# Retention and two wide feed-forward layers on one core: moving the first layer's float64 loads to GpSimd's queue, and three smaller moves of loads and operand making

## The chip, the cores and the metric

The kernel runs on one core of a Trainium2 chip. The metric is device time in microseconds, start to end of one execution on that core. Engine names are those of the profile: PE is TensorE (matmul) and PEld its weight loads, DVE is VectorE, ACT is ScalarE, POOL is GpSimd, and SP is SyncE, which here only issues DMAs. A DMA that SP or ACT issues goes out on queue q1 or q10 of the profile, a DMA that POOL issues on q0.

## The reference

```python
# q, k, v: 4 x 8 x 768 x 64 float32; x: 3072 tokens x 512; w_in 512 x 2048, w_out 2048 x 512 in float64
gamma = 1.0 - 2.0 ** (-5.0 - np.arange(H))
for t in range(S):                                   # retention, per batch and head
    state = gamma * state + k[t] (outer) v[t]
    y[t] = q[t] @ state / sqrt(64)
x = y.transpose(0, 2, 1, 3).reshape(3072, 512)
h = x @ moe_w_in;  x = (h * sigmoid(1.702 * h)) @ moe_w_out
h = x @ moe2_w_in; x = square(max(h, 0)) @ moe2_w_out
```

## The kernel before

**Retention.** The 3072 tokens are 24 units of 128 tokens. `load_unit` brings one unit as two transfers of 512 KB from SP's queue into one of four buffers (`UNITS = 4`). In iteration u the loop runs `scores(u)` on PE (16 matmuls), `outputs(u - 1)` (yp, dp and the matmuls with the state), then `cv_step`, and last issues the load of unit u + 3, whose buffer is free once `outputs(u - 1)` has read unit u - 1. `masked` (pt) and `scaled` (x) are the two DVE operations that each unit needs. Of the six blocks of 512 tokens, block 0 is split into hi and lo parts at once, blocks 1 to 3 stay in SBUF (`XHELD = 4`), and blocks 4 and 5 go to a DRAM tensor `xkept`, one store of 256 KB per unit from POOL's queue.

**The first layer's weights.** They come as float64 words: 32 slices (`order`) of 512 KB. A slice is a load into one of three `raw` buffers (`cv_load`, line 114, SP's queue), a scaling on ACT (`cv_a`, tile `hm`), and a chain of five or six DVE operations with one ACT copy (`cv_step`, lines 152 to 176) that leaves the tile `w` with a hi and a lo part. The load of slice n + 3 needs the buffer of slice n and so waits for that slice's last DVE operation, line 176. Some slices are made in the retention, the others beside block 0 of the first layer.

**The first layer, blocks 0 to 3** (`NSTD = 4`). For each of 16 column groups f, `up` runs 12 matmuls into `h`, ACT makes `gs` and `gh`, DVE makes `gl` (line 590), and `down` of the group two earlier (`LOOK = 2`) runs 12 matmuls into `y`. Beside blocks 1 to 3, `background(BG)` gives a generator (`maker`) a credit per group, in estimated us of DVE: it makes the operands of the second half of the program, 16 sets of sums from the first layer's weights (`make_first`, tiles `wh`) and 32 jobs on the second layer's float64 weights (`make_second`, tiles `w`, `hm`, `wq`, stored to `kw` by POOL). In block 3 the generator `x_operands` also runs, one step per group from f = 5 on: it makes the operands `xh`, `xl` of the first seven-product block.

**Seven-product blocks.** The last third of the first layer and all of the second run as four blocks of 1024 tokens with seven products in place of eight (`up2`, `down2`; L748 is their matmul). Their weight tiles `r` come by SP's queue in 256 KB loads from `kw`, each used by six matmuls, up to eight ahead (`SLOTS = 8`, of which two are free before block 3 ends). At the start of each block `x_loads` loads the next block's x (four transfers of 512 KB on POOL's queue, line 623); `up2` calls `background(BGUP)` 14 times.

All orders of work are written out by hand: an engine runs its instructions in the order in which the program issues them, and so does each queue.

Of the kernel before, what the change touches and what calls it, by code (L numbers as in the profile page):

```python
# [18 lines left out]
P = 128  # L19
# [21 lines left out]
SLOTS = 8  # L41
EARLY = 2
BG = 4.3
BGUP = 2.0

# [7 lines left out]
def tile_retention_then_two_ffns(  # L55
# [22 lines left out]
        ctx.enter_context(tc.tile_pool(name=f"wr{i}", bufs=1, side="right", reuse_waits="tile"))  # L78
        for i in range(EARLY)
    ]  # L80
    cv_ctx = ctx.enter_context(ExitStack())
    cv_p = cv_ctx.enter_context(tc.tile_pool(name="cv", bufs=2, side="right"))
    maker_ctx = ctx.enter_context(ExitStack())
# [20 lines left out]
    def cv_load():  # L104
        n = cv["load"]
        if n == len(order):
            return
        if n >= cv["b"] + 3:
            return
        cv["load"] += 1  # L110
        f, s = order[n]
        raw = cv_p.tile([P, 512, 2], U32, tag="raw", name=f"raw{n}", bufs=3)
        src = w1[f, :, s * 512:(s + 1) * 512].bitcast(U32)
        nc.sync.dma_start(out=raw, in_=src.rearrange("p (c t) -> p c t", t=2))
        cvt[n] = [raw]

    def cv_a():
# [230 lines left out]
            yield from low(*last)  # L348

    def make():  # L350
        cv_ctx.close()
        raw_p.append(maker_ctx.enter_context(
            tc.tile_pool(name="k0", bufs=2, side="right", reuse_waits="tile")
        ))
        yield from make_first()
        yield from make_second()
# [36 lines left out]
    with tc.manual_schedule():  # L393

        with (
# [13 lines left out]
            table_sb = att.tile([P, 1], F32, tag="table", name="table_sb", bufs=1)  # L409
            nc.scalar.activation(out=table_sb, in_=warm_sb[:, 0:1], func=ACTF.Gelu_apprx_sigmoid)  # L410


            x0_sb = [att.tile([P, NP, P], F32, tag="x0", name="x0_0")]
            st_sb = [att.tile([P, NP, P], F32, tag=f"st{i}", name=f"st{i}", bufs=1) for i in range(2)]
            for t in st_sb:
                nc.gpsimd.memset(t, 0.0)
# [67 lines left out]
            def outputs(u):  # L484
                t = units.pop(u)
                pt, vs = pend.pop(u)
                b, c = divmod(u, CPB)
                qk = t[:, 0:1024].rearrange("p (b n a i) -> p b n a i", b=2, n=2, a=2)
                kn = t[:, 1024:1536].rearrange("p (h e) -> p h e", h=H)
                yp = aps.tile([P, NP, P], F32, tag="yp", name=f"yp{u}")  # L490
                for p in range(NP):
                    for r in range(2):
                        nc.tensor.matmul(  # L493
                            yp[64 * r:64 * r + 64, p, :], vs[:, 2 * p + r, :], pt[:, r, p, :],
                            start=(p == 0), stop=(c == 0), skip_group_check=True,
                        )
                dp, st = state.pop(b, (None, None))
                if c == 0:
                    dp = aps.tile([P, 2, NP, D], F32, tag="dp", name=f"dp{b}")
                if c < CPB - 1:  # L500
                    for p in range(NP):
                        for r in range(2):
                            nc.tensor.matmul(
                                dp[64 * r:64 * r + 64, 0, p, :], kn[:, 2 * p + r, :], vs[:, 2 * p + r, :],
                                start=(c == 0 and p == 0), stop=(c == CPB - 2), skip_group_check=True,
                            )
                    ns = st_sb[u % 2]
                    for r in range(2):
                        h = slice(64 * r, 64 * r + 64)
                        nc.scalar.copy(out=ns[h, :, h], in_=dp[h, 0])  # L510
                    state[b] = (dp, ns)
                if c > 0:
                    for p in range(NP):
                        nc.tensor.matmul(
                            yp[:, p, :], st[:, p, :], qk[:, p // 2, 0, p % 2, :],
                            start=False, stop=True, skip_group_check=True,
                        )
                j, o = divmod(u, UPB)
                cols = slice(o * P, (o + 1) * P)
                if 0 < j < XHELD and o == 0:  # L520
                    xs[j] = block_tiles(f"x{j}")

                def scaled():
                    if 0 < j < XHELD:
                        for i in range(2):
                            pair = slice(2 * i, 2 * i + 2)
                            v.tensor_tensor(
                                out=xs[j][i][:, :, cols], in0=yp[:, pair], in1=ytab_sb[c][:, pair], op=ALU.mult
                            )
                        return  # L530
                    xt = x0_sb.pop() if x0_sb else att.tile([P, NP, P], F32, tag="x0", name=f"x0_{u}")
                    v.tensor_tensor(out=xt, in0=yp, in1=ytab_sb[c], op=ALU.mult)
                    if j == 0:
                        pend["x"] = (xt, cols)
                    else:
                        nc.gpsimd.dma_start(out=xkept[j][:, :, cols], in_=xt)

                return scaled

# [9 lines left out]
            for u in range(NU + 1):  # L549
                masked = scores(u) if u < NU else None  # L550
                split_0()
                scaled = outputs(u - 1) if u > 0 else None
                if 0 < u < CPB:
                    for p in range(NP):
                        nc.scalar.mul(ytab_sb[u][:, p, :], ytab_sb[0][:, p, :], ystep_sb[:, u, p:p + 1])
                cv_step(2 * WA if u >= 3 and u % 2 != 1 or u == 3 else 0, masked, scaled, u >= 2)
                if u > 0:
                    load_unit(u + UNITS - 1)

# [13 lines left out]
        def up(n, f):  # L573
            hi, lo = weights(f, 0)
            hp = hp_p.tile([P, TB], F32, tag="h", name=f"h{n}_{f}")
            for k in range(KD):
                xh, xl = hl[n][k]
                nc.tensor.matmul(hp, lo[:, k], xh, start=(k == 0), stop=False)  # L578
                nc.tensor.matmul(hp, hi[:, k], xh, start=False, stop=False)  # L579
                nc.tensor.matmul(hp, hi[:, k], xl, start=False, stop=(k == KD - 1))  # L580
            g = g_p.tile([P, TB], F32, tag="gs", name=f"gs{n}_{f}", bufs=1)
            gh = g_p.tile([P, TB], F32R, tag="gh", name=f"gh{n}_{f}")
            gl = g_p.tile([P, TB], F32R, tag="gl", name=f"gl{n}_{f}")

            nc.scalar.activation(out=g, in_=hp, func=ACTF.Gelu_apprx_sigmoid)  # L585
            nc.scalar.copy(out=gh, in_=g)  # L586
            gs[n, f] = (gh, gl)

            def low():
                v.tensor_tensor(out=gl, in0=g, in1=gh, op=ALU.subtract)  # L590

            if n == 0:
                cv_step(len(order), None, low)
                if f % 3 == 2:
                    cv_step()
            else:
                low()
                if f < NF - 1:
                    background(BG)

        def down(n, f):
            hi, lo = weights(f, 1)
# [99 lines left out]
        for n in range(NSTD):  # L702
            for f in range(NF):
                up(n, f)
                if f >= LOOK:
                    down(n, f - LOOK)
                elif n > 0 and f == 0:
                    down(n - 1, NF - 1)
                    finish(n - 1)
                if f == 2 and XHELD - 2 <= n < NSTD - 2:  # L710
                    xs[n + 2] = load_block(f"x{n + 2}", xkept[n + 2])
                if n == NSTD - 1:
                    if f == 3:
                        gen = x_operands(*x_loads(*blocks[0]))
                    if f >= 5:
                        next(gen, None)
                    if f == NF - 3:
                        fetch()
            down(n, NF - 2)
            if n + 1 < NSTD:  # L720
                split_x(n + 1, xs.pop(n + 1))
# [25 lines left out]
        def matmul(a, w, b, start, stop):  # L747
            nc.tensor.matmul(a, w, b, start=start, stop=stop, skip_group_check=True)  # L748

        def up2(l, n, first):  # L750

            xb, yb, zb = {}, {}, {}
            late = deque()
# [24 lines left out]
                    v.scalar_tensor_tensor(out=t, in0=t, scalar=0.0, in1=t, op0=ALU.max, op1=ALU.mult)  # L778

            for p in range(NQ + 1):  # L780
                if p < NQ:
                    xb[p] = bank(f"X{l}_{n}_{p}")
                    product(1, p, xb[p][0], True)
                    copy(gt(11, p), xb[p][0])
                else:
                    next(first)
# [156 lines left out]

        for k, (l, n) in enumerate(blocks):
            todo.extend((i, m) for i in ORDER for m in range(NQ // 2))
            gen = iter(())
            if k + 1 < len(blocks):
                gen = x_operands(*x_loads(*blocks[k + 1]))
            rest = down2(l, n, lambda: next(gen, None))
            up2(l, n, rest)  # L950
            for _ in rest:
                pass
            for _ in gen:
                pass
            if (l, n) == (1, 0):
                assert next(maker, 0) == 0 and not acts
# [82 lines left out]
```

## Time and profile before

| | us |
|---|---|
| runs shown (3): lowest, median, highest | 1087.12, 1088.05, 1088.72 |
| the profiled execution: its own time | 1089.05 |
| its span, first to last instruction | 1087.3 |
| PE busy | 1057.3 |
| DVE busy | 795.3 |
| ACT busy | 512.2 |
| POOL busy | 83.7 |

The profiled execution took 1.0 us more than the median of the runs, and its span is 1.75 us shorter than its own time. PE busy is time in which at least one matmul is under way; at a lower clock the same matmul is busy for longer.

### The profile page before, as it was taken

Reading aid. Unit: us, or ns where it says so; the run is one execution under the profiler, and the core shown is the slowest. Engines: PE = TensorE matmul, PEld = TensorE weight load, DVE = VectorE, ACT = ScalarE, POOL = GpSimd, SP = SyncE. Lnnn points to the kernel's source line nnn. Section 1 sums busy time; section 2 is a strip of 40 time slices with the busy share of each in tenths; the row PEclk is TensorE's granted clock in tenths of the full one; section 3 lists DMA queues with packets and bytes.
Section 4 is the critical chain, followed back from the end, with each engine's and each line's share of the span. In section 5 each row is a group of like instructions: output and inputs, shape, how many; then the busy total and the mean of one; then the engine's idle time right before and its main releaser. Section 6 shows DMA issues by size and latency. Waiting matters only on the chain.

```text
span 1087.3 us, 15308 instructions
## 1 busy us (share of the span) xinstructions
PE 1057.3 (97%) x5482; PEld 875.9 (81%) x5482; DVE 795.3 (73%) x1197; ACT 512.2 (47%) x862; POOL 83.7 (8%) x117
## 2 busy tenths in 40 slices
PE   7888999999999999899999999999999999999998
PEld 6877887888888888778888878888888888888886
DVE  3877998869798789945788667698444888355953
ACT  4877554434444445444546433446323455224443
POOL 2001000011111121110000110000100000000000
PEclk8999999999999999989999999999999999999999
DMA  8898445986466596599966798766876667767664
GB/s 310 300 328 297 156 136 169 385 336 228 180 215 221 165 337 211 195 344 327 308 208 206 236 334 273 210 214 205 260 244 195 194 210 232 215 193 194 195 211 165
DMA packets 107004, 259.34 MB, mean 239 GB/s; under 512 B 11312, under 2 KB 11440, under 8 KB 106928
## 3 DMA queue, kind: packets, MB, share of 16 engines
q1 hardware_dynamic: 83696, 173.42, 49.9%
q0 software_dynamic: 18048, 67.12, 17.0%
q10 hardware_dynamic: 5184, 17.83, 5.0%
q8 instruction: 44, 0.72, 0.3%
q14 instruction: 32, 0.26, 0.1%
HBM read 184.91 MB, written 73.40 MB: 238 GB/s over the span
## 4 chain that ended last, share of the span: by engine, by line
PE 82%; DMA 9%; DVE 6%; ACT 1%; issue 1%; SPq 0%; POOL 0%; DVEq 0%; ACTq 0%; POOLq 0%
PE D L748 28%; PE X L748 15%; PE Z L748 7%; PE h L578 4%; PE y L610 4%; PE h L580 4%; PE h L579 4%; PE y L609 4%; PE y L608 4%; DMA unit<-qkv 4%; PE Y L748 4%; DMA r<-kw 3%; PE yp L493 1%; PE sc L444 1%; DMA raw<-win 1%
## 5 line engine op out<-in xcount | busy, mean ns | idle before, releaser
L748 PE MATMUL D<-gx,r 128*128 128x512 f32 x1344 | 306.4, 389 | 0.0
L748 PEld LDWEIGHTS D<-gx,r 128*128 128x128 f32 x1344 | 252.0, 188 | 53.0 <-DVE gx L849 0.8
L849 DVE TENSOR_TENSOR gx<-g,gx 128x1024 fp32r<-128x1024 f32 x112 | 136.5, 1221 | 36.9 <-ACT gx L848 36.7
L748 PE MATMUL X<-xh,r 128*128 128x512 f32 x512 | 159.0, 392 | 3.2 <-DMA r<-kw 3.2
L848 ACT CAST gx<-g 128x1024 fp32r<-128x1024 f32 x112 | 116.7, 1053 | 92.9 <-PE D L748 83.3
L769 ACT COPY g<-X 128x512 f32<-128x512 f32 x96 | 56.5, 588 | 186.7 <-PE X L748 186.7
L774 DVE TENSOR_TENSOR g<-Z,g 128x512 f32<-128x512 f32 x64 | 44.2, 691 | 126.8 <-ACT g L769 92.3
L748 PEld LDWEIGHTS X<-xh,r 128*128 128x128 f32 x512 | 96.0, 189 | 26.1 <-issue 2.5
L610 PE MATMUL y<-gl,w 128*128 128x512 f32 x256 | 100.7, 393 | 3.2 <-DVE gl L590 3.2
L578 PE MATMUL h<-hl,w 128*128 128x512 f32 x256 | 99.8, 390 | 1.9 <-DVE w L176 1.9
L608 PE MATMUL y<-gh,w 128*128 128x512 f32 x256 | 100.3, 392 | 0.0
L609 PE MATMUL y<-gh,w 128*128 128x512 f32 x256 | 100.3, 392 | 0.0
L748 PE MATMUL X<-xl,r 128*128 128x512 f32 x256 | 99.9, 390 | 0.0
L579 PE MATMUL h<-hl,w 128*128 128x512 f32 x256 | 99.6, 389 | 0.0
L580 PE MATMUL h<-hl,w 128*128 128x512 f32 x256 | 99.6, 389 | 0.0
L748 PE MATMUL Z<-xh,r 128*128 128x512 f32 x256 | 79.0, 390 | 0.3 <-DMA r<-kw 0.3
L586 ACT CAST gh<-gs 128x512 fp32r<-128x512 f32 x64 | 40.0, 624 | 62.1 <-PE y L609 61.3
L585 ACT ACTIVATE gs<-h 128x512 f32<-128x512 f32 x64 | 38.2, 597 | 56.5 <-PE h L580 37.3
L590 DVE TENSOR_TENSOR gl<-gs,gh 128x512 fp32r<-128x512 f32 x64 | 44.0, 688 | 27.8 <-ACT gh L586 27.5
L610 PEld LDWEIGHTS y<-gl,w 128*128 128x128 f32 x256 | 48.5, 190 | 13.6 <-DVE gl L590 3.6
L578 PEld LDWEIGHTS h<-hl,w 128*128 128x128 f32 x256 | 48.1, 188 | 12.2 <-DVE w L176 2.3
L609 PEld LDWEIGHTS y<-gh,w 128*128 128x128 f32 x256 | 48.5, 189 | 10.2
(103 smaller groups left out, 1586.5 us busy)
## 6 DMA issues: line engine op xcount, KB each, us to landing
r<-kw SPq DMA_DIRECT2D x448, 256.0 KB, 3.0
kw<-wq POOLq DMA_DIRECT2D x32, 896.0 KB, 6.2
unit<-qkv SPq DMA_DIRECT2D x47, 512.0 KB, 7.3
raw<-w SPq DMA_DIRECT2D x32, 512.0 KB, 3.7
kw<-wh POOLq DMA_DIRECT2D x16, 1024.0 KB, 5.1
kw<-w SPq DMA_DIRECT2D x16, 512.0 KB, 6.5
raw<-win ACTq DMA_DIRECT2D x16, 512.0 KB, 5.1
raw<-wout ACTq DMA_DIRECT2D x16, 512.0 KB, 5.4
```

What stands on the lines that cost most here:

```text
L578: nc.tensor.matmul(hp, lo[:, k], xh, start=(k == 0), stop=False)
L579: nc.tensor.matmul(hp, hi[:, k], xh, start=False, stop=False)
L580: nc.tensor.matmul(hp, hi[:, k], xl, start=False, stop=(k == KD - 1))
L590: v.tensor_tensor(out=gl, in0=g, in1=gh, op=ALU.subtract)
L608: nc.tensor.matmul(a, lo[:, e], gh, start=s0, stop=False)
L609: nc.tensor.matmul(a, hi[:, e], gh, start=False, stop=False)
L610: nc.tensor.matmul(a, hi[:, e], gl, start=False, stop=s1)
L748: nc.tensor.matmul(a, w, b, start=start, stop=stop, skip_group_check=True)
L769: nc.scalar.copy(out=t, in_=a)
L774: v.tensor_tensor(out=t, in0=a, in1=t, op=ALU.add)
L848: nc.scalar.copy(out=hi, in_=src)
L849: v.tensor_tensor(out=lo, in0=src, in1=hi, op=ALU.subtract)
```

## The change

- The loads of the first layer's float64 slices are issued by POOL instead of SP.
- Units 5 and 9 of the retention get a slice to make as well; beside block 0 the extra slices come after groups 3, 6 and 9 in place of 2, 5, 8, 11 and 14.
- Blocks 4 and 5 of x are kept in SBUF (`xout`) in the retention; two stores of 1 MB each, at groups 2 and 3 of block 0, take the place of eight of 256 KB.
- The next block's x is loaded in the middle of the up projection of a seven-product block (p = 4 of 8), not at the block's start.
- In block 3 of the first layer, groups 5 to 14 give `maker` a credit of 2.9 in place of 4.3; `BGUP` is 2.3 in place of 2.0.

```diff
-BGUP = 2.0
+BGUP = 2.3
...
+    keep_ctx = ctx.enter_context(ExitStack())
+    keep_p = keep_ctx.enter_context(tc.tile_pool(name="keep", bufs=1, side="right"))
+    xout = {j: keep_p.tile([P, KD, TB], F32, tag=f"xo{j}", name=f"xout{j}") for j in range(XHELD, NT // TB)}
...
-        nc.sync.dma_start(out=raw, in_=src.rearrange("p (c t) -> p c t", t=2))
+        nc.gpsimd.dma_start(out=raw, in_=src.rearrange("p (c t) -> p c t", t=2))
...
     def make():
+        while cv["b"] < len(order):
+            cv_step()
         cv_ctx.close()
+        keep_ctx.close()
...
-                        return
-                    xt = x0_sb.pop() if x0_sb else att.tile([P, NP, P], F32, tag="x0", name=f"x0_{u}")
-                    v.tensor_tensor(out=xt, in0=yp, in1=ytab_sb[c], op=ALU.mult)
-                    if j == 0:
+                    elif j > 0:
+                        v.tensor_tensor(out=xout[j][:, :, cols], in0=yp, in1=ytab_sb[c], op=ALU.mult)
+                    else:
+                        xt = att.tile([P, NP, P], F32, tag="x0", name=f"x0_{u}")
+                        v.tensor_tensor(out=xt, in0=yp, in1=ytab_sb[c], op=ALU.mult)
                         pend["x"] = (xt, cols)
-                    else:
-                        nc.gpsimd.dma_start(out=xkept[j][:, :, cols], in_=xt)
...
-                cv_step(2 * WA if u >= 3 and u % 2 != 1 or u == 3 else 0, masked, scaled, u >= 2)
+                cv_step(2 * WA if u >= 3 and (u % 2 != 1 or u in (3, 5, 9)) else 0, masked, scaled, u >= 2)
...
                 cv_step(len(order), None, low)
-                if f % 3 == 2:
+                if f in (3, 6, 9):
                     cv_step()
...
-                    background(BG)
+                    background(BG if n < NSTD - 1 or f < 5 else BG - 1.4)
...
+                if n == 0 and f in (2, 3):
+                    j = XHELD + f - 2
+                    nc.gpsimd.dma_start(out=xkept[j], in_=xout[j])
...
-        def up2(l, n, first):
+        def up2(l, n, first, loads):
...
             for p in range(NQ + 1):
+                if p == NQ // 2:
+                    loads()
...
-            gen = iter(())
-            if k + 1 < len(blocks):
-                gen = x_operands(*x_loads(*blocks[k + 1]))
-            rest = down2(l, n, lambda: next(gen, None))
-            up2(l, n, rest)
+            gen = [iter(())]
+
+            def loads():
+
+                if k + 1 < len(blocks):
+                    gen[0] = x_operands(*x_loads(*blocks[k + 1]))
+
+            rest = down2(l, n, lambda: next(gen[0], None))
+            up2(l, n, rest, loads)
```

PE's order is the same instruction for instruction. On SP, early in the retention, the queue before has the slice loads (`raw`, L114) among the units' (L435):

```order
L435 DMA unit_225<-qkv 128x1024 x2
L114 DMA raw_278<-w 128x1024
L114 DMA raw_280<-w 128x1024
L435 DMA unit_282<-qkv 128x1024 x2
L114 DMA raw_337<-w 128x1024
L435 DMA unit_339<-qkv 128x1024 x2
L114 DMA raw_403<-w 128x1024
```

In the change SP's queue holds units alone there (L440 is the same line), and POOL's queue has the slice loads among the multiplications of V (`vs`, units 2 to 5), which POOL does for the first six units:

```order
L468 TENSOR_TENSOR vs_243<-unit_172,tab_sb 128x512
L118 DMA raw_283<-w 128x1024
L118 DMA raw_285<-w 128x1024
L468 TENSOR_TENSOR vs_300<-unit_175,tab_sb 128x512
L118 DMA raw_342<-w 128x1024
L468 TENSOR_TENSOR vs_357<-unit_230,tab_sb 128x512
L118 DMA raw_408<-w 128x1024
L468 TENSOR_TENSOR vs_423<-unit_287,tab_sb 128x512
L118 DMA raw_476<-w 128x1024
```

So nothing but units waits on SP now, and the slice loads wait behind one another on POOL. On DVE, at the end of block 3, before the change one job of `maker` (`w`, `hm`, `wq`) stands between the `gl` of two groups; these rows are from group 13's `gl` to group 14's (`xl` is the step of `x_operands`):

```order
L590 TENSOR_TENSOR gl_13_4315<-gs_13_4313,gh_13_4314 128x512
L342 TENSOR_TENSOR w_21_4238<-w_21_4238 128x128
L343 TENSOR_TENSOR w_21_4238<-w_21_4238 128x128
L318 TENSOR_SCALAR w_22_4325<-hm_22_4237 128x512
L323 SCALAR_TENSOR_TENSOR w_22_4325<-hm_22_4237,w_22_4325 128x512
L327 TENSOR_SCALAR hm_22_4237<-w_22_4325 128x512
L329 SCALAR_TENSOR_TENSOR hm_22_4237<-raw_22_4272,hm_22_4237 128x512
L637 TENSOR_TENSOR xl_4105<-xb_2_1_0_3858,xh_4104 128x1024
L590 TENSOR_TENSOR gl_14_4365<-gs_14_4363,gh_14_4364 128x512
```

and with the change, from group 14's `gl` to group 15's, the last that PE waits for before the seven-product blocks:

```order
L594 TENSOR_TENSOR gl_14_4322<-gs_14_4320,gh_14_4321 128x512
L333 SCALAR_TENSOR_TENSOR hm_20_4197<-raw_20_4189,hm_20_4197 128x512
L301 TENSOR_TENSOR wq_4281<-w_19_4198,wq_4281 128x7x128
L340 TENSOR_TENSOR w_20_4283<-w_20_4283,hm_20_4197 128x512
L343 TENSOR_TENSOR w_20_4283<-w_20_4283 128x128
L344 TENSOR_TENSOR w_20_4283<-w_20_4283 128x128
L642 TENSOR_TENSOR xl_4253<-xb_2_0_0_3848,xh_4252 128x1024
L594 TENSOR_TENSOR gl_15_4362<-gs_15_4360,gh_15_4361 128x512
```

By the end of block 3 `maker` has come to job 20 in place of job 23; the jobs left over are made in the seven-product blocks.

## Rows read from the trace of the kernel before

**Rows 1.** Busy us (instructions) by stretch of PE, PEld, DVE, ACT, POOL; clock; DMA share; GB/s.
```profile
0.00:50.00 50.00, 40.72 (x518) 34.86 (x520) 30.55 (x61) 29.81 (x96) 7.80 (x13) 0.90 0.86 306
50.00:100.00 50.00, 41.89 (x600) 38.11 (x596) 37.86 (x65) 36.86 (x124) 2.99 (x4) 0.93 0.93 323
...
300.00:400.00 100.00, 100.00 (x443) 82.81 (x442) 84.80 (x173) 46.42 (x72) 17.32 (x20) 1.00 0.67 221
```

**Rows 2.** PE's waits over the span: for what, us in total, times, longest.
```profile
PE sc L444 <- DMA unit<-qkv: 14.0, 7, 3.9
PE y L610 <- DVE gl L590: 3.2, 1, 3.2
PE X L748 <- DMA r<-kw: 3.2, 8, 1.0
PE h L578 <- DVE w L176: 1.9, 1, 1.9
```

**Rows 3.** Waits of SP's queue from 0 to 115 us: the largest.
```profile
SPq L114 <- DVE w L176: 47.2, 10, 8.2
```

**Rows 4.** SP's issues in order of time: start us, us, queue and line.
```profile
30.96 0.33 SPq L114 DMA_DIRECT2D raw<-w  x1
31.38 2.05 SPq L435 DMA_DIRECT2D unit<-qkv  x4
```

**Rows 5.** Busy time by stretch, as Rows 1, 10 us each in the retention.
```profile
20.00:30.00 10.00, 9.43 (x150) 8.65 (x152) 7.91 (x18) 8.28 (x27) 2.44 (x3) 1.00 0.96 366
30.00:40.00 10.00, 7.63 (x96) 6.72 (x93) 9.36 (x19) 7.23 (x26) 0.00 (x0) 0.90 0.80 273
```

**Rows 6.** DMA from 0 to 110 us: totals; POOL's stores with time to landing.
```profile
DMA packets 9664, 34.03 MB, mean 309 GB/s; under 512 B 1097, under 2 KB 1225, under 8 KB 9650
...
xkept<-x POOLq DMA_DIRECT2D x7, 256.0 KB, 6.0
```

**Rows 7.** Chain that ended last, in the retention: start us, us, what.
```profile
12.34 1.98 PE yp L493 x16
...
101.25 1.09 PE sc L444 x16
...
104.91 1.09 PE sc L444 x16
...
110.69 0.24 PE h L578
```

**Rows 8.** DVE in order of time, block 0: two slices made back to back.
```profile
188.02 0.68 DVE L176 SCALAR_TENSOR_TENSOR w<-raw,hm 128x512 fp32r<-128x512 f32 x1
...
191.45 0.69 DVE L176 SCALAR_TENSOR_TENSOR w<-raw,hm 128x512 fp32r<-128x512 f32 x1
```

**Rows 9.** Chain that ended last, block 3: DVE's part of group 7.
```profile
415.93 0.60 DVE gl L590
```

**Rows 10.** DVE in order of time: the last group of block 3.
```profile
461.23 0.69 DVE L590 TENSOR_TENSOR gl<-gs,gh 128x512 fp32r<-128x512 f32 x1
```

**Rows 11.** Busy time by stretch, as Rows 1, around the end of block 3.
```profile
455.00:460.00 5.00, 3.78 (x17) 2.81 (x15) 4.83 (x11) 1.22 (x2) 0.97 (x1) 1.00 0.62 220
460.00:465.00 5.00, 3.03 (x7) 2.45 (x8) 3.65 (x5) 0.59 (x1) 0.03 (x1) 0.63 0.46 165
465.00:470.00 5.00, 5.00 (x17) 3.88 (x17) 0.69 (x1) 1.82 (x3) 3.04 (x6) 0.69 0.78 254
```

**Rows 12.** DMA queues, 632 to 644 us: packets, MB, share of 16 engines.
```profile
q1 hardware_dynamic: 1314, 2.39, 52.4%
q0 software_dynamic: 518, 1.92, 40.3%
```

**Rows 13.** DMA issues of the whole span: times, KB, median us to landing.
```profile
kw<-wq POOLq DMA_DIRECT2D x32, 896.0 KB, 6.2
...
raw<-w SPq DMA_DIRECT2D x32, 512.0 KB, 3.7
```

**Rows 14.** DMA issues, 466 to 478 us: one store from POOL's queue.
```profile
kw<-wq POOLq DMA_DIRECT2D x1, 896.0 KB, 14.4
```

More of the change, by code (lines that the diff above doesn't have):

```diff
@@ L410, in tile_retention_then_two_ffns @@
             nc.scalar.activation(out=table_sb, in_=warm_sb[:, 0:1], func=ACTF.Gelu_apprx_sigmoid)
-            x0_sb = [att.tile([P, NP, P], F32, tag="x0", name="x0_0")]
             st_sb = [att.tile([P, NP, P], F32, tag=f"st{i}", name=f"st{i}", bufs=1) for i in range(2)]
@@ L945, in tile_retention_then_two_ffns @@
             todo.extend((i, m) for i in ORDER for m in range(NQ // 2))
-            gen = iter(())
-            if k + 1 < len(blocks):
-                gen = x_operands(*x_loads(*blocks[k + 1]))
-            rest = down2(l, n, lambda: next(gen, None))
-            up2(l, n, rest)
+            gen = [iter(())]
[4 more added lines that the diff above has]
+            up2(l, n, rest, loads)
             for _ in rest:
                 pass
-            for _ in gen:
+            for _ in gen[0]:
                 pass
```

## The prediction

> **What bounds the kernel now.** I read the busy time by stretch first [rows 1]. Away from the edges PE is the bound: from 300 to 400 us it is busy 100.00 of 100, at full clock, with 443 matmuls recorded, which is 100 / 443 = 0.226 us each and 24 x 0.226 = 5.42 us per column group of the first layer. There nothing but fewer matmuls would help, and PE's order does not change, so the change can only win back PE's gaps. The first 100 us hold the largest: PE is busy 40.72 + 41.89 us, so idle 17.4. The list of PE's waits [rows 2] names the owners: 14.0 us for units in the retention, and three smaller ones, 3.2 us for the last `gl` of block 3, 3.2 us for `r` tiles, and 1.9 us for a slice of the first layer's weights beside block 0. The change has one edit for each. (A measurement of this kernel can tell a change of about 0.2%, 2.2 us, from none.)
>
> **The retention: slice loads off SP's queue, x kept in SBUF.** Why do units come late? In part DMA is full: from 20 to 30 us the engines are 0.96 busy and move 366 GB/s. But from 30 to 40 us they are only 0.80 busy, at 273 GB/s, and there PE is idle 2.4 us [rows 5]. SP's rows show what held them: units 7 and 8 go out at 31.38 us, straight behind a slice load at 30.96 [rows 4] that had waited for a slice's last DVE operation. Such waits on SP add up to 47.2 us in ten [rows 3], and each stands ahead of units whose buffers may be free. With the slice loads on POOL that wait is gone from the units' way, though not from the slices'; behind it on POOL stand only later slices and, early, `vs` of units 3 to 5, which PE needs an iteration later.
>
> What is late next is DMA itself. Bytes hardly change: 34.03 MB went by in the first 110 us [rows 6]; the eight `xkept` stores (2.1 MB, most of them in that time) leave, two more slices (1.0 MB) come in. The last unit's scores start at 104.91 us, the first layer at 110.69 [rows 7]. So some 32.4 MB (309 GB/s x 104.9) must move before the last scores. Ends: at the rate of before and a few hundred KB less I count 1 us won. At the best stretch's 366 GB/s they would be there by 89 us, and PE would bound: a unit takes it 104.91 - 101.25 = 3.66 us at full clock, 24 of them 88 us, and from 12.34 us on that gives about 101 for the retention's end [rows 7], 9.7 us won. I take a rate between: per full share DMA moves 306 / 0.86 = 356 and 323 / 0.93 = 347 GB/s in the two halves of the first 100 us [rows 1], and a share of 0.94, just under the 0.96 of the best stretch, makes that 330. 32.4 MB then take 98.2 us, **6.7 us** less; the share should hold since the four unit buffers keep up to three units in flight once SP no longer stops. The two extra slices are hidden: DVE is busy 68 us of the first 100 [rows 1] and a slice is 191.45 - 188.02 = 3.4 us [rows 8]. Without that cover they would cost 6.8.
>
> The Trainium skill speaks against this term (Trainium Kernel Development and Optimization, Key Constraints): DMAs issued from SP, ACT and POOL share the same 16 engines, and issuing from several only saves the sequencer's issue time. By that rule alone the gain would be the low end, 1 us. The trace differs as far as SP's rows go: what SP loses is 47.2 us of waiting, not of issuing.
>
> **Block 0: two slices fewer, and earlier.** The order listing shows 13 slices made in the retention in place of 11 (not fourteen), so 19 are left beside block 0 in place of 21. The wait of 1.9 us [rows 2] came where a slice was made in the group just ahead of the matmul that uses it; its last operation ended at 188.02 + 0.68 = 188.70 us [rows 8]. Now extras come after groups 3, 6 and 9, and that slice is made a group (5.42 us) earlier, more than the 1.9 that it was late. I take **1.9**, ends 0 and 1.9. The two 1 MB stores go out while DMA is far from full and no engine waits for them.
>
> **End of block 3.** From group 7 to group 15 DVE's `gl` moves from 415.93 to 461.23 us [rows 9, 10], 5.66 us per group where PE needs 5.42; DVE falls behind and PE stands for 3.2 us. The clock falls too: mean granted 0.63 and 0.69 of full in the next ten us, that is mostly 1.2 GHz. PE's matmuls from 455 to 470 us are 17 + 7 + 17 = 41 where 15 / 0.226 = 66 would fit [rows 11]: 25 x 0.226 = **5.7 us** lost, wait and clock together. The change takes 1.4 us of DVE credit from each of ten groups, to about 4.3 us, below 5.42; DVE keeps up and I count all 5.7, ends 2.5 and 5.7. The 14 us of work taken out, less the 8.4 that two blocks' higher `BGUP` takes up early (28 x 0.3), falls into later calls, where DVE is less full.
>
> **`r` tiles.** Eight waits, 3.2 us [rows 2], fall some 15 us into the first two seven-product blocks, where DMA runs full: from 632 to 644 us SP's queue moved 2.39 MB and POOL's 1.92 [rows 12]. PE needs 0.26 MB per six matmuls (1.36 us), 193 GB/s; it got 199, barely that, and had no tiles ahead left. There x loads (2.1 MB) met stores of the block before. In the middle of `up2` there are no such stores, but `maker` is faster. I take half, **1.6 us**, ends 3.2 and -1 (the burst stops PE again, as long as before, with 1 us more for one more store).
>
> **Sum.** 6.7 + 1.9 + 5.7 + 1.6 = 15.9 us off. The profiled execution took 1089.05 us, so 1073.15 in its terms; the median of the runs is 1.0 lower, so I predict **1072 us**. All high ends give 9.7 + 1.9 + 5.7 + 3.2 = 20.5, so 1067.5; all low ends 1 + 0 + 2.5 - 1 = 2.5, so 1085.5.
>
> **Rivals.**
> - **DMA-bound retention.** The bytes are what they were and the queue's stops were only where the shortage showed. For it: 0.93 busy from 50 to 100 us [rows 1]. Against: 0.80 at 30 to 40. Retention gives 1, the sum 10.2, the time 1088.05 - 10.2 = 1077.8. Chance 0.20. The Trainium skill's rule on queues (Trainium Kernel Development and Optimization, Key Constraints) would lead here.
> - **The wait moves on with the work.** DVE still falls behind at the end of block 3 (5.7 not won), since its work per group is more than the credits say. For it: the credit 4.3 and 5.66 measured per group. Against: 1.4 off leaves 1.1 us of slack per group. 15.9 - 5.7 = 10.2, so 1077.8 again. Chance 0.08.
> - **Slower: slices late from POOL's queue.** Three `raw` buffers go round, so three slices cannot take less than one landing plus the 3.4 us that a slice takes DVE. Beside block 0, 19 slices have 16 x 5.42 = 86.7 us, 4.56 each, so the point is a landing of 3 x 4.56 - 3.4 = 10.3 us. SP's 512 KB slices land in 3.7 us, POOL's 896 KB stores in 6.2 [rows 13], and one in 14.4 [rows 14]. At 14.4 a slice takes (14.4 + 3.4) / 3 = 5.9 us, 19 of them 113, 26 more than now; less the other 14.0, the time is 1088.05 + 12 = 1100. Against: DMA is half idle there. Chance 0.05. The Trainium skill (SBUF — State Buffer, SBUF: two separate sides) has a reason for such landings: GpSimd writes a DMA's descriptors through a port that some DVE operations hold. POOL's 6.2 us median, with DVE busy 85 of 100 us, shows no delay beyond the size of the stores, so I leave the chance low.
> - **No change.** Several of these at once, within 2.2 us: 0.05.
>
> The forecast has the remaining 0.62. Faster by over 0.2% is 0.62 + 0.20 + 0.08 = 0.90, within 0.2% 0.05, slower 0.05. For 8 in 10 the range takes in the forecast's ends and the first two rivals, with 3 us for the latter's other terms: **1067 to 1081**. The forecast's own range is 1067 to 1077.
>
> **What would show it.** Right: SP waits for no DVE operation in the retention; the first `h` matmul starts at 102 to 105 us; DMA share from 20 to 90 us is above 0.95; no wait of `h` for `w`; no PE wait for `gl` at the end of block 3 and granted clock 1.00 there; under 2 us of waits for `r`, now some 15 us past the middle of an up projection. Wrong: units still late with DMA near full (first rival); DVE at the end of block 3 still over 5.42 us per group (second); ACT's `hm` waiting for `raw`, and PE for `w` beside block 0 (third).

## The result, and the profile after

The changed kernel takes 1075.12 us (median of 4 runs, 1074.34 to 1075.82), the kernel before, run beside it, 1088.35. The ratio is 0.9882, with a 95% interval of 0.986 to 0.9904: faster by 1.2%. The forecast was 1072.0, in a range of 1067 to 1081. The profiled execution took 1074.34 us with a span of 1072.6, which is 14.7 less than the span before.

The page's first part, busy time by engine over the span:

```profile
PE 1053.4 (98%) x5482; PEld 873.4 (81%) x5482; DVE 795.2 (74%) x1197; ACT 510.8 (48%) x862; POOL 94.7 (9%) x143
```

Where did the 14.7 us come from? Matmuls in PE's order of time are the milestones. The first `h` matmul, which is the end of the retention, starts at 104.03 us where it started at 110.45, so 6.4 us were won up to there. The last `h` starts at 443.93 in place of 452.50, 2.2 more. The first matmul of the seven-product part starts at 452.32 in place of 466.40, 5.5 more around the end of block 3. The remaining 600 us bring 0.6.

PE's waits over the span, in the columns of [rows 2]:

```profile
PE sc L449 <- DMA unit<-qkv: 5.7, 6, 1.9
PE yp L498 <- DVE pt L458: 3.2, 3, 2.5
PE Y L756 <- DMA r<-kw: 1.8, 2, 1.4
PE X L756 <- DMA r<-kw: 1.2, 3, 0.5
...
PE Z L756 <- DMA r<-kw: 0.7, 2, 0.4
```

The waits for units fell from 14.0 to 5.7 us. The wait of `h` for a slice and that of `y` for `gl` are gone. The waits for `r` are what they were: 1.8 + 1.2 + 0.7 = 3.7 us, where `X` had 3.2 [rows 2] and `Z` another 0.3 before. And there is a large new one in the retention: 3.2 us of `yp` for `pt`, which DVE makes. The largest waits of SP's queue from 0 to 110 us:

```profile
SPq L440 <- PE yp L519: 48.1, 16, 6.6
SPq L261 <- DVE w L180: 31.3, 1, 31.3
```

The 47.2 us for `w` [rows 3] have become waits for PE, which frees a unit's buffer; that is the limit that the buffers themselves set. The one long wait for `w` that is left (31.3 us) belongs to a store of finished slices to `kw`, issued behind the last unit, and holds no unit up.

The retention in stretches of 10 us, in the columns of [rows 1]:

```profile
20.00:30.00 10.00, 9.45 (x154) 8.60 (x151) 7.94 (x18) 7.90 (x27) 1.03 (x1) 1.00 1.00 380
30.00:40.00 10.00, 7.54 (x62) 6.70 (x63) 10.00 (x21) 8.55 (x28) 2.32 (x3) 0.70 0.80 288
40.00:50.00 10.00, 9.84 (x155) 8.88 (x154) 10.00 (x20) 7.94 (x27) 1.06 (x2) 0.96 0.89 299
50.00:60.00 10.00, 9.78 (x147) 8.82 (x145) 10.00 (x21) 8.19 (x26) 1.06 (x2) 1.00 1.02 401
60.00:70.00 10.00, 8.72 (x141) 7.94 (x141) 10.00 (x19) 9.86 (x35) 0.72 (x2) 1.00 1.00 384
...
80.00:90.00 10.00, 8.64 (x132) 7.61 (x130) 9.79 (x17) 8.38 (x30) 0.53 (x1) 1.00 1.00 348
```

From 50 to 90 us DMA is full; over 20 to 90 us its share is 0.96, as forecast, but with 0.80 and 0.89 in the middle. From 30 to 70 us the third busy figure, DVE's, is 10.00 of 10. In the stretch from 30 to 40 us, [rows 5] of before, nothing improved: PE is busy 7.54 us, DMA 0.80, and the granted clock fell to 0.70 of full (0.90 before).

At the end of block 3, the same columns:

```profile
450.00:455.00 5.00, 5.00 (x23) 4.14 (x23) 3.33 (x7) 1.76 (x3) 1.14 (x2) 1.00 0.58 147
455.00:460.00 5.00, 5.00 (x23) 4.13 (x23) 0.75 (x2) 1.80 (x4) 0.00 (x0) 1.00 1.01 382
```

PE has no gap, the clock stays at 1.00 (2.4 GHz) where it had fallen to 0.63 [rows 11]. DVE in order of time, its last two `gl` of block 3:

```profile
442.12 0.69 DVE L594 TENSOR_TENSOR gl<-gs,gh 128x512 fp32r<-128x512 f32 x1 [1.15 <-ACT gh L590]
...
447.56 0.69 DVE L594 TENSOR_TENSOR gl<-gs,gh 128x512 fp32r<-128x512 f32 x1 [0.88 <-ACT gh L590]
```

They are 5.44 us apart, PE's pace, and DVE now stands idle ahead of each (1.15 and 0.88 us, for ACT).

### The profile page after: what moved, and what is told of

It is laid out like the page before. It is cut to its first block, busy times and chain, and to the rows that moved or that the text cites. A ratio compares the mean times of both kernels' runs of the same rounds, so it can differ in the third digit from the quotient of the medians.

```text
span 1072.6 us, 15314 instructions
## 1 busy us (share of the span) xinstructions
PE 1053.4 (98%) x5482; PEld 873.4 (81%) x5482; DVE 795.2 (74%) x1197; ACT 510.8 (48%) x862; POOL 94.7 (9%) x143
## 4 chain that ended last, share of the span: by engine, by line
PE 87%; DMA 8%; issue 3%; ACT 1%; POOL 0%; SPq 0%; DVE 0%; POOLq 0%; ACTq 0%
PE D L756 28%; PE X L756 14%; PE Z L756 7%; PE y L613 5%; PE h L582 5%; PE h L583 5%; PE h L584 5%; PE y L614 5%; PE y L615 5%; DMA r<-kw 4%; PE Y L756 4%; DMA unit<-qkv 3%; ACT vs L473 1%; DMA raw<-w 1%; PE yp L498 1%
## 5 line engine op out<-in xcount | busy, mean ns | idle before, releaser
L756 PEld LDWEIGHTS Z<-xh,r 128*128 128x128 f32 x256 | 47.8, 188 | 11.7 <-DVE wq L301 0.8
L584 PEld LDWEIGHTS h<-hl,w 128*128 128x128 f32 x256 | 48.1, 188 | 10.1
L756 PEld LDWEIGHTS X<-xl,r 128*128 128x128 f32 x256 | 48.1, 188 | 10.0
```

## The experiments

Ratios are to the kernel before on the same chip; diffs are against the changed kernel unless the text says otherwise. "The retention's end" is the start of the first `h` matmul in the profiled execution: 110.45 us before, 104.03 changed. It differs between executions of one code. Four profiles with the changed retention (the change, and below the x loads at the start, the credits undone and the x loads before the down projection) have 104.0, 106.5, 103.7 and 104.2; six with eleven slices in it, loaded from POOL's queue (below), 95.4 to 100.4. So 3 us between two single profiles show nothing, and the two groups do not overlap.

### The queue: put the slice loads back on SP

```diff
-        nc.gpsimd.dma_start(out=raw, in_=src.rearrange("p (c t) -> p c t", t=2))
+        nc.sync.dma_start(out=raw, in_=src.rearrange("p (c t) -> p c t", t=2))
```

> The changed kernel with the slice loads back on SP's queue, all else as changed. My theory: the slices' waits for DVE stand ahead of units again, SP loses some 40 us or more to them, PE waits for units over 10 us, the retention ends at 108 to 111 us and the time is 4 to 6.5 us above the changed kernel's 1075.1, so 1079 to 1081.5. Rival (full DMA and the stores taken out made the gain, not the queue): the retention still ends within 1.5 us of 104.3 and the time stays within 1.5 us of 1075.

Measured: 1082.06 us (1080.82 to 1084.31), ratio 0.9948 (0.9933 to 0.9964), about 7 us slower than the change. The retention ends at 114.46, in the profile of the execution of 1084.31 us. PE's longest waits:

```profile
PE sc L449 <- DMA unit<-qkv: 13.8, 11, 3.8
```

and SP's from 0 to 110 us:

```profile
SPq L118 <- DVE w L180: 42.6, 9, 9.4
SPq L118 <- DVE top L158: 16.0, 3, 8.1
```

The waits for units are back at 13.8 us, and so are SP's stops behind DVE. With thirteen slices on SP's queue the retention is even 4 us longer than before. The theory of the queue held; the time and the retention's end lie 0.6 and 3.5 us above its ranges.

### The queue alone: the kernel before, with only its slice loads on POOL

Against the kernel before:

```diff
-        nc.sync.dma_start(out=raw, in_=src.rearrange("p (c t) -> p c t", t=2))
+        nc.gpsimd.dma_start(out=raw, in_=src.rearrange("p (c t) -> p c t", t=2))
```

> The kernel before with one edit, the slice loads on POOL's queue: 11 slices, stores per unit, x at the block's start, credits as before. My theory (the queue gives nearly all of the retention's gain, and the two extra slices gave part of it back): the retention ends at 95 to 100 us in place of 110.5, PE's wait for a slice beside block 0 (1.9 us), the wait for gl (3.2) and those for r (3.2) stay, and the time is 10 to 15 us below the kernel before's, 1073 to 1078. Rival (the stores kept in SBUF or the extra slices are needed for it): the retention ends at 103 us or later and the time is 1080 or more.

Measured: 1077.87 us (1075.57 to 1080.28), ratio 0.9903 (0.9878 to 0.9927), with 1087.61 before beside it: 9.7 us from one word. The retention ends at 100.38, 10.1 us earlier than before and 3.7 earlier than in the change, though the profile is of the slowest execution (1080.28 us). PE's waits:

```profile
PE sc L444 <- DMA unit<-qkv: 7.3, 6, 2.5
PE X L748 <- DMA r<-kw: 2.6, 6, 0.6
PE y L610 <- DVE gl L590: 2.5, 1, 2.5
PE h L578 <- DVE w L176: 1.9, 1, 1.9
```

The waits of the other edits stay, as they should. So the queue alone wins more in the retention than the whole change does there; something else in the change gives a part back. The time lies in the range of the theory, the retention's end 0.4 us outside it.

Did the transfers get faster on two queues? No: a unit lands a median of 7.5 us after its issue here and in the change, 7.3 before, and a slice 7.2 us here, 5.4 before (0 to 110 us). What fell is the time that units stood behind slices before they were issued: the slices' waits for `w`, 47.2 us on SP before [rows 3], are gone from its list.

### x stores from the retention again

```diff
-                        v.tensor_tensor(out=xout[j][:, :, cols], in0=yp, in1=ytab_sb[c], op=ALU.mult)
+                        xt = att.tile([P, NP, P], F32, tag="x0", name=f"x0_{u}")
+                        v.tensor_tensor(out=xt, in0=yp, in1=ytab_sb[c], op=ALU.mult)
+                        nc.gpsimd.dma_start(out=xkept[j][:, :, cols], in_=xt)
```

(and the tiles `xout` with their two late stores left out)

> The changed kernel with the stores of blocks 4 and 5 as before: eight of 256 KB from POOL's queue in the retention's last third, in place of two of 1 MB in block 0. My theory (in the changed kernel DMA is 1.00 busy from 50 to 90 us, so bytes count there): 1.5 to 2 MB more to move at some 360 GB/s, the retention ends 3 to 6 us later than 104.0 and the time is 3 to 6 us above 1075.1. Rival (DVE sets the pace there, at 10.0 of 10 us from 30 to 70): the end moves by under 1.5 us, and so does the time.

Measured: 1075.07 us (1074.76 to 1075.83), ratio 0.9891 (0.9869 to 0.9913). The retention ends at 106.25, within what its code scatters. The theory, which gave the stores 3 to 6 us, missed. The rival held for the time; the end moved 2.2 us where it allowed 1.5. Keeping x in SBUF is worth nothing that shows in the time. Why is not shown: units still wait for DMA in both profiles (5.7 us in the change, 7.1 here).

### Slices as before: eleven in the retention

```diff
-                cv_step(2 * WA if u >= 3 and (u % 2 != 1 or u in (3, 5, 9)) else 0, masked, scaled, u >= 2)
+                cv_step(2 * WA if u >= 3 and (u % 2 != 1 or u == 3) else 0, masked, scaled, u >= 2)
...
-                if f in (3, 6, 9):
+                if f % 3 == 2:
```

> The changed kernel with the slices' places of before: 11 in the retention and extras after groups 2, 5, 8, 11 and 14 of block 0. The forecast had the two extra slices hidden in the retention: then its end stays at 104.3 us within 0.5, the wait for a slice beside block 0 returns with up to 1.9 us, and the time is 1 to 2 us above 1075.1. Rival (DVE is busy 10.0 of 10 us from 30 to 70 us in the changed kernel, so the extra slices cost there): the retention ends 1.5 to 4 us earlier, and with the wait of 1.9 us in block 0 the time is 0 to 2 us below 1075.1.

Measured: 1071.01 us (1069.61 to 1073.29), ratio 0.9846 (0.9829 to 0.9864), 4.1 us less than the change in the median, and its slowest run is faster than the change's fastest. The retention ends at 95.39; beside block 0 the old wait is back:

```profile
PE h L582 <- DVE w L180: 1.9, 1, 1.9
```

So the two extra slices were not hidden. They buy 1.9 us in block 0 and cost more than that in the retention. The rival named this, but took the retention's end for 1.5 to 4 us earlier; here it is 8.6. A part of that may be scatter: from 10 to 20 us the granted clock is 1.00 in this profile, 0.66 in the change's and 0.69 in that of the next run.

### Eleven slices, and the extras of block 0 earlier

```diff
-                cv_step(2 * WA if u >= 3 and (u % 2 != 1 or u in (3, 5, 9)) else 0, masked, scaled, u >= 2)
+                cv_step(2 * WA if u >= 3 and (u % 2 != 1 or u == 3) else 0, masked, scaled, u >= 2)
...
-                if f in (3, 6, 9):
+                if f in (1, 3, 5, 7, 9):
```

> The changed kernel with 11 slices in the retention (units 4, 6, 8 and so on) and the five extras beside block 0 after groups 1, 3, 5, 7 and 9. My theory: the retention ends near the 95.4 us of the run with the places of before (1071.0), and the wait for the slice, two waits of PE's weight loads with 4.2 us there, is gone since that slice is made a group earlier: 1067 to 1069.5. Rival (DVE cannot keep up beside block 0 with 21 slices in any order): a wait for a slice or for gl of 1.5 us or more stays and the time is 1070 to 1072.

Measured: 1068.40 us (1067.71 to 1069.38), ratio 0.983 (0.9807 to 0.9852), below the interval of the change. The retention ends at 98.43, and no `h` waits for a slice. The 1.9 us can be had beside block 0 without a slice more in the retention. DVE's `pt` in order of time shows what a slice costs where; in the changed kernel:

```profile
33.08 1.21 DVE L458 TENSOR_TENSOR pt<-sc,tab_sb 128x1024 f32<-128x1024 f32 x1
37.69 1.22 DVE L458 TENSOR_TENSOR pt<-sc,tab_sb 128x1024 f32<-128x1024 f32 x1
41.02 1.22 DVE L458 TENSOR_TENSOR pt<-sc,tab_sb 128x1024 f32<-128x1024 f32 x1
44.08 1.22 DVE L458 TENSOR_TENSOR pt<-sc,tab_sb 128x1024 f32<-128x1024 f32 x1
48.68 1.23 DVE L458 TENSOR_TENSOR pt<-sc,tab_sb 128x1024 f32<-128x1024 f32 x1
53.28 1.23 DVE L458 TENSOR_TENSOR pt<-sc,tab_sb 128x1024 f32<-128x1024 f32 x1
```

and with eleven slices:

```profile
31.31 1.23 DVE L458 TENSOR_TENSOR pt<-sc,tab_sb 128x1024 f32<-128x1024 f32 x1
34.37 1.23 DVE L458 TENSOR_TENSOR pt<-sc,tab_sb 128x1024 f32<-128x1024 f32 x1
37.70 1.24 DVE L458 TENSOR_TENSOR pt<-sc,tab_sb 128x1024 f32<-128x1024 f32 x1
```

With a slice in every second unit DVE takes 37.70 - 31.31 = 6.4 us for two units, no more than PE, whose units take 3.66 [rows 7] or, in the profile of the run just above, 3.20 (scores from 72.11 to 75.31 us). Where units with slices follow each other, DVE takes 4.6 us for one (44.08, 48.68, 53.28), and PE waits for `pt`. The edit `u in (3, 5, 9)` filled exactly the gaps: it makes units 3 to 6 and 8 to 10 such runs.

The two extra slices are also 1.0 MB more to load, 3.1 us at the 339 GB/s that DMA moved up to the last scores of the changed kernel. Could that be the cost, and not DVE? Busy time with eleven slices, in the columns of [rows 1]:

```profile
30.00:40.00 10.00, 8.65 (x132) 7.66 (x128) 10.00 (x22) 9.31 (x32) 2.24 (x3) 1.00 0.97 348
40.00:50.00 10.00, 10.00 (x156) 9.19 (x156) 9.13 (x17) 9.66 (x33) 0.53 (x1) 1.00 1.00 372
```

In these 20 us the changed kernel's DMA is only 0.80 and 0.89 busy, while its DVE is full and SP waits for PE to free units' buffers. So there the bytes were not the limit. What they cost behind 50 us, where DMA is full, no run separates.

### Thirteen slices, the extras in later units

```diff
-                cv_step(2 * WA if u >= 3 and (u % 2 != 1 or u in (3, 5, 9)) else 0, masked, scaled, u >= 2)
+                cv_step(2 * WA if u >= 3 and (u % 2 != 1 or u in (3, 15, 19)) else 0, masked, scaled, u >= 2)
```

> The changed kernel with its 13 slices in the retention, but the two extra ones at units 15 and 19 in place of 5 and 9. If the extra slices cost so much because they stand in the stretch where DVE also splits block 0's x (units 4 to 10): the retention ends at 100 us or before and the time is 2 to 4 us below 1075.1. If any two more slices cost their 6.8 us of DVE: it ends at 102 to 105 and the time stays within 1.5 us of 1075.1.

Measured: 1072.31 us (1071.72 to 1076.24), ratio 0.9873 (0.9845 to 0.99). The retention ends at 100.38, as late as the latest of the group with eleven slices, and the median is 2.8 us below the change's. That fits the place as the main cost, with the same bytes and the same number of slices; but the ranges overlap (the change has 1074.34 to 1075.82), so the shares of place and number are not settled.

### Less operand making beside block 3, undone

```diff
-BGUP = 2.3
+BGUP = 2.0
...
-                    background(BG if n < NSTD - 1 or f < 5 else BG - 1.4)
+                    background(BG)
```

> The changed kernel with the maker's credits of before (4.3 in all groups of block 3, 2.0 in the up projections). My theory: DVE takes over 5.5 us per group again, PE waits 2 to 4 us for the last gl of block 3, the clock falls behind it, and the time is 4 to 6 us above 1075.1. Rival (the lag came from a late start that the retention's gain has removed): no wait for gl over 1 us and the time within 1 us of 1075.1.

Measured: 1079.07 us (1076.33 to 1084.83, six runs), ratio 0.9929 (0.9903 to 0.9956), 4 us slower than the change in the median; the two intervals just touch. Among PE's waits:

```profile
PE y L615 <- DVE gl L594: 5.1, 2, 3.6
```

and busy time from 400 to 470 us in the columns of [rows 1] (in the change PE has 69.60 of 70 at clock 1.00):

```profile
400.00:470.00 70.00, 64.90 (x279) 52.81 (x278) 60.21 (x108) 35.73 (x53) 8.63 (x10) 0.98 0.66 227
```

The wait for `gl` returns, and PE has 4.7 us less of the 70.

### The x loads at the start of an up projection again

```diff
+            loads()
             for p in range(NQ + 1):
-                if p == NQ // 2:
-                    loads()
```

> The changed kernel with the next block's x loaded at the block's start again. My theory by the forecast's sum: the waits of PE for r tiles come to some 3.5 us or more, all within 25 us of the start of the first two seven-product blocks, and the time is 1 to 2 us above 1075.1. Rival (the changed kernel's own waits for r are 3.7 us in total, against 3.5 before, so the move only shifted them): the waits come to 3 to 4.5 us and the time stays within 0.8 us of 1075.1.

Measured: 1077.36 us (1075.08 to 1080.49), ratio 0.9905 (0.9883 to 0.9926), which overlaps the change's. The profile is of the slowest execution, 1080.49 us; PE's waits in it:

```profile
PE Z L756 <- DMA r<-kw: 3.6, 3, 1.6
...
PE X L756 <- DMA r<-kw: 2.6, 6, 0.7
```

That is 6.2 us for `r`, where the change has 3.7. But the profiles with x at the start have 3.5 (before), 4.1 (the queue alone) and these 6.2, those with x in the middle and the change's credits 2.4 to 4.3. By the waits the move may be worth something, by the times it can't be told.

### The x loads between up and down

```diff
-                if p == NQ // 2:
+                if p == NQ:
                     loads()
```

> The changed kernel with the next block's x loaded at the end of the up projection (p = 8), where the maker stores nothing any more. My theory (x loads stop PE only where they meet the maker's stores of 0.9 MB): PE's waits for r fall from 3.7 us to under 1.5 and the time is 1.5 to 3 us below 1075.1. Rival (any burst of 2.1 MB uses up the eight tiles ahead): the waits stay at 3 to 4.5 us, now at the start of the down projections, and the time within 0.8 us of 1075.1.

Measured: 1074.89 us (1073.29 to 1078.81), ratio 0.9894 (0.9858 to 0.9929), as the change. PE's waits:

```profile
PE D L756 <- DMA r<-kw: 2.6, 3, 1.0
...
PE Z L756 <- DVE w L340: 0.8, 1, 0.8
```

The waits went along to the down projection `D`, with 0.8 us for a late `w` of DVE's. At 2.6 us they lie between the theory's 1.5 and the rival's 3. And the edit did not do what the theory wanted, x loads away from `maker`'s stores: POOL's order of time shows such a store of 0.9 MB straight ahead of them.

```profile
516.82 0.94 POOL L302 DMA_DIRECT2D kw<-wq  x1 [9.63 <-DVE wq L301]
517.75 2.14 POOL L628 DMA_DIRECT2D xb<-ykept  x4
```

In the changed kernel it is the same for its first two bursts of x loads (the second at 640.67); the third, at 764.48, comes after `maker`'s last store (671.84):

```profile
485.75 0.93 POOL L302 DMA_DIRECT2D kw<-wq  x1 [11.50 <-DVE wq L301]
486.66 2.18 POOL L628 DMA_DIRECT2D xb<-ykept  x4
...
764.48 2.11 POOL L628 DMA_DIRECT2D xb<-ykept  x4
```

PE's waits for `r` within 20 us of the three bursts are 2.1, 0.9 and 0.4 us (another 0.4 stands ahead of the first). The last is one wait in PE's order of time:

```profile
778.34 0.71 PE L756 MATMUL X<-xh,r 128*128 128x512 f32 x2 [0.36 <-DMA r<-kw]
```

Behind that third burst no profile here has more than 0.4 us. So the place within a block does not matter much, but a burst alone costs little: the waits come where it meets `maker`'s loads and stores.

### The four x transfers one by one

Against the version with eleven slices and early extras:

```diff
-                if p == NQ // 2:
-                    loads()
+                if 2 <= p < 6:
+                    loads(p - 2)
```

(`loads(i)` issues the i-th of the four transfers, and the last makes the generator)

> The kernel with 11 slices in the retention and early extras (1068.4 us), with the four transfers of the next block's x spread: one each at p = 2, 3, 4 and 5 of the up projection in place of all four at p = 4. My theory (the waits for r come from 2.1 MB at once in a stretch where the tiles and the maker already take most of DMA): PE's waits for r fall from 3.2 us to under 1.5 and the time to 1065.5 to 1067.5. Rival (the maker's stores alone, 0.9 MB each, are enough to use up the eight tiles): the waits stay at 2.5 us or more and the time at 1067.5 to 1069.

Measured: 1068.36 us (1066.81 to 1069.28), ratio 0.9813 (0.979 to 0.9837): the same as without it, and above the 1067.5 that the theory allowed. PE's list has no wait for `r` any more, but this one:

```profile
PE X L756 <- ACT g L777: 2.3, 1, 2.3
```

ACT in order of time at its place (in brackets the idle time before, and who ended it):

```profile
502.41 0.66 ACT L295 ACTIVATE hm<-raw 128x512 f32<-128x512 f32 x1 [5.11 <-DMA raw<-wout]
```

and PE:

```profile
503.60 0.73 PE L756 MATMUL X<-xh,r 128*128 128x512 f32 x2 [2.33 <-ACT g L777]
```

ACT stood 5.11 us at an `hm` whose load was late, and `g`, which frees PE's accumulator, stood behind it. POOL still issues a 0.9 MB store of `maker` straight ahead of x loads (468.37 us, and two x loads at 469.32), and PE no longer waits: it took the burst and `maker`'s traffic together. In this profile 2.3 us of what that gave went into a wait on ACT's queue.

### That `hm` later in its generator

Against the run before, `scale(n + 1)` (which issues `hm`) is called after a piece's own work, not ahead of it:

```diff
-                scale(n + 1)
                 raw = raws[n]
...
                 yield 0.7
+                scale(n + 1)
                 if last is not None:
```

> The kernel with spread x loads (1068.4 us, no wait for r, but ACT stood 5.1 us at the scaling of a second-layer load and PE 2.3 us behind it), with that scaling placed half a job later on ACT, after the next load's issue. My theory (ACT reaches the scaling half a job after the load went out, and the spread x loads make the load late): the 2.3 us of PE behind ACT vanish, no wait for r returns, the time is 1064.5 to 1067. Rival (the stall only moves, to DVE waiting for the scaled tile or to another load): PE loses 1.5 us or more in the seven-product blocks and the time is 1067 to 1069.5.

Measured: 1064.29 us (1062.62 to 1067.97), ratio 0.9801 (0.9771 to 0.983), the fastest of all, clearly below the change (0.986 at the least). PE's waits:

```profile
PE sc L449 <- DMA unit<-qkv: 4.8, 6, 1.9
...
PE yp L498 <- POOL vs L468: 0.7, 1, 0.7
PE Z L756 <- DMA r<-kw: 0.5, 1, 0.5
PE y L615 <- DVE gl L594: 0.3, 1, 0.3
```

Behind the retention 0.8 us of listed waits are left. Against the version just before it the interval overlaps, so only the vanished 2.3 us wait is shown, not a gain in time of its own.

### One `vs` more on ACT

Against that fastest version:

```diff
-                if u < CPB:
+                if u < CPB - 1:
```

> The kernel of the run with the later scaling, with the V multiplication of unit 5 on ACT in place of POOL, where it stands behind the fourth slice's load, which waits for a slice's last DVE operation (7.5 us idle on POOL). My theory (this wait is the one that moving the slices to POOL's queue added, and PE pays for it): PE's wait for vs on POOL, 1.1 to 2.3 us in the runs so far, vanishes and the time falls by 0.5 to 2 us. Rival (DMA sets the retention's end anyway): the end of the retention and the time stay within 0.5 us.

Measured: 1064.57 us (1063.06 to 1066.58), ratio 0.9793 (0.977 to 0.9817): no difference. The wait of `yp` for POOL's `vs` fell from 0.7 to 0.4 us, and `yp` waits 1.0 us for ACT's `ytab` in its place. The rival held.

## Why the prediction came out right, point by point

**Retention: 6.7 predicted, 6.4 measured, right in size and wrong in two steps.** That SP's queue held units behind slices is shown from both sides: the loads back on SP cost 7 us, the loads alone moved to POOL win 9.7. The last scores start at 98.42 us (chain of waits), where 32.4 MB at 330 GB/s gave 98.2. By then 33.4 MB had moved, at 339 GB/s, so both numbers were 3% low and cancel. And two steps were off, in opposite directions. "The two extra slices are hidden: DVE is busy 68 us of the first 100" failed: an average over 100 us does not show that DVE is at 10.00 of 10 from 30 to 70. The profiled retention ends some 5 to 9 us earlier without them (98.43 and 95.39 against 104.03). And the high end of 9.7, from PE's pace of 3.66 us times 24 and an end at "about 101", was no floor: 95.39 was reached. Not all 24 units take PE 3.66 us, some take 3.20. The agreement in size is partly luck: more won at the queue, and a part of it lost at DVE.

**Block 0: 1.9 predicted, 2.2 measured** between the first and the last `h` matmul. The wait is gone, and it returns with the old places of the extras (1.9 us).

**End of block 3: 5.7 predicted, 5.5 measured**, clock included. Undoing the credits brings the wait for `gl` back at 5.1 us and costs 4 us in the median.

**`r` tiles: 1.6 predicted, nothing measured.** This is the mis-sized term: 3.5 us of waits before, 3.7 after. The step that failed is "In the middle of `up2` there are no such stores". There are none of the block before, but `maker` stores there, 0.9 MB in the microsecond ahead of the x loads. Four x transfers in one burst, beside `maker`'s traffic, take the share that `r` needs: at the start, in the middle and before the down projection. Beside `maker` but spread out they leave no such wait; in a burst but behind `maker`'s end they leave 0.4 us at most. So the forecast's mechanism, x loads that meet stores, was half the cause, and its new place did not avoid them. The low end of this term ("the burst stops PE again") had the case.

**Sum.** 14.7 us in the profiled executions and 13.2 between medians (1088.35 - 1075.12), against 15.9. The difference of 2.7 is the `r` term and scatter of the retention's end.

**The first rival** (DMA-bound retention, 1 us) is out: DMA is now full from 50 to 90 us, but at 348 to 401 GB/s, and the end still moved. The Trainium skill says (Trainium Kernel Development and Optimization, Key Constraints) that issuing from several engines only saves the sequencer's issue time. The queue alone gave 9.7 us here, so the measurement decides against it: on a queue that is served in order, a load that waits for its buffer holds back others whose buffers are free.

**The second rival** (DVE still behind at block 3) is out by the `gl` rows. **The third** (slices late from POOL) needed landings of 10.3 us beside block 0. They are 5.3 there (SP's were 3.7 [rows 13]); ACT's `hm` waits 3.6 us in all for `raw`, but PE's `h` never for `w`. From the list of DMA issues from 104 to 190 us:

```profile
raw<-w POOLq DMA_DIRECT2D x17, 512.0 KB, 5.3
```

That `xkept` stores take part in the retention's shortage was in the sum as bytes only; the run with the stores put back shows no effect on the time.

## What to carry to other kernels

Look at a DMA queue's own waits, and at what stands behind each: loads that wait for a slow consumer belong on a queue whose next entries are not urgent. Before work is called hidden on an engine, look at that engine in stretches as short as the work, and at whether the work comes in consecutive iterations: with a slice in every second unit DVE kept PE's pace, with slices in units running it did not. A prefetch that is issued as one burst cost little where the stream beside it had DMA to itself, and stopped PE where other stores ran too, at each of three places; there, issue it piece by piece, and then look for the queue that the gain went to.

## What was not expected of the hardware

One DVE operation in the changed retention takes three times as long as its like. DVE in order of time:

```profile
31.30 1.26 DVE L156 TENSOR_SCALAR raw<-hm 128x512 uint32<-128x512 uint32 x1
```

and POOL:

```profile
31.14 1.13 POOL L468 TENSOR_TENSOR vs<-unit,tab_sb 128x512 f32<-128x512 f32 x1
```

The median of that DVE form is 0.429 us. It starts 0.16 us after POOL's `vs` and ends 0.29 us after it, 0.83 later than it should. A maximum of 1.26 to 1.28 us stands in all five profiles that have a slice in unit 5 and load it from POOL's queue, and none above 0.50 in the others (0.43 with the same slices loaded from SP). The Trainium skill (SBUF — State Buffer, SBUF: two separate sides) says that VectorE in some modes and GpSimd share a pair of ports as an exclusive lock, where whoever starts first makes the other block; these rows agree, though no run here varied the mode. So a slice's early operations can also meet POOL's work, at 0.8 us; it shows once in each of these five profiles.

DMA moved 401 GB/s from 50 to 60 us of the changed retention and 384 in the next ten, above the 366 that the sum took for the best that this load would give [rows 5].
